# Eight weight sums on VectorE instead of adding DMAs, a PSUM bank for each partial result of a down product, a wider margin in the list scheduler

## The chip, the cores and the metric

One NeuronCore of a Trainium2 chip runs the whole kernel. The metric is the device time of one execution in microseconds. Five engines work side by side, each on its own queue in order: TensorE (PE: matmuls from SBUF into PSUM), VectorE (DVE), ScalarE (ACT), GpSimd (POOL) and SyncE (SP). POOL and SP also issue DMAs: SP the loads and stores, POOL the DMAs that add into SBUF.

## The reference

A gated linear attention over four batches, eight heads, 768 steps and 48 channels, and a bilinear feed-forward layer on its output:

```python
f = 1.0 / (1.0 + np.exp(-f_logit))
for t in range(S):                                  # S = 768
    state = f[:, :, t, :, None] * state + np.einsum('bhd,bhe->bhde', k[:, :, t], v[:, :, t])
    y[:, :, t] = np.einsum('bhd,bhde->bhe', q[:, :, t], state)
x = y.transpose(0, 2, 1, 3).reshape(B * S, H * D)   # 3072 tokens x 384
a = x @ w_a                                         # 384 x 1536
b = x @ w_b
out = (a * b) @ w_out                               # 1536 x 384
```

All matmuls are in fp32. The weights come as doubles and are turned into fp32 on the chip.

## The kernel before

The tokens are cut into eight blocks of 384. A block needs two *units* of attention (four heads each; sixteen units, 0 to 15). Of a unit, DVE makes running products of `f` and scales `q` and `k` (`f_in`, `q_in`, `k_in`; two ACT sigmoids and one POOL step `inv` go ahead of it), PE makes scores (L364), transposes of k (L399), state gains (L423) and the two parts of the output (L466 from the chunk itself, L487 from the states). DVE masks the scores (`at`, L387), ACT copies the transposes (`kT`, L409) and the output (`y`, L512), and SP stores `y` into `xT`, the block's input to the feed-forward layer, and then loads f, k, q and v of the unit three further on.

The feed-forward layer of blocks 0 and 1 is plain: an *up product* (L567) is six matmuls for one of twelve groups of 128 columns, three for b and three for a; ACT copies b, DVE multiplies (L589). For the later blocks the up products are a fast scheme with 15 products for 18 (`up_triples`, L687), and all *down products* (`down`, L780) are one with 7 for 8 in the manner of Strassen and Winograd: two groups of 128 tokens at a time, twelve times in all. Both schemes want sums of weight blocks:

- `combine_w_out`: t1, t2, t4 in the buffer `spare`, and the block b12 of `w_out` changed in place (it is t3);
- `combine_w_ba`: six sums in the buffer `raw` (here called s[0] to s[5]), and after them two blocks of `w_ba`, a31 and a22, changed in place. They may change only when all up products of blocks 0 and 1 are through and when the sums that read them have read them.

These sums are made by ACT, which writes a first term with its sign, and by DMAs of POOL's queue that add one more term each (`add_by_dma`, L599): 20 adding DMAs and 12 ACT copies (L602).

What stands behind what on each engine is decided at build time. `main` holds the feed-forward work in order. Each step has an engine, an assumed duration and, for some, the beat of PE (four matmuls of 164 ns) by which it should be through, its due time. Five lines (`for_out`, `for_x`, `core`, `fore`, `for_ba`) hold the weights' sums on w_out, the sums of x, the units' attention, the work ahead of it, and the weights' sums on w_ba. Before each step of `main`, `fill` puts in what is ready on those lines, unless `delays` finds that a step of `main` on the same engine would come too late for its due time, with `LATENCY` of 200 ns as margin; at marked places a line is emptied up to a point, ready or not.

A down product has four partial results of 192 columns: x0, x1, m0 and m1. PE makes them in the order x0 (3 beats), m1, x0 again (added), x1, m0, x1 anew, m0 again (added). ACT copies x0 to `u` (L797), m1 to `o` (L804) and x0 to `o` (L807); DVE adds the rest. x0 and x1 share one PSUM bank of 512 columns, m0 and m1 another; two down products behind each other take turns with four banks. `up_triples` goes round the same four banks, called v, u, r and t there.

Of the kernel before, what the change touches and what calls it, by code (L numbers as in the profile page):

```python
# [17 lines left out]
ALU = mybir.AluOpType  # L18
# [114 lines left out]
def by_quotients(ctx, tc, q, k, f_logit, v, moe_w_a, moe_w_b, moe_w_out, out, ident, weights, bad):  # L133
    nc = tc.nc
# [26 lines left out]
    for i in range(NSET):  # L161
        t = {n: fixed([128, 2, BLK], f"{n}_in{i}") for n in "qkf"}
# [109 lines left out]
    PE, DVE, ACT, POOL, SP = range(5)  # L272
# [64 lines left out]
    ps_f = [ps_a.tile([128, 512], FP32, tag=f"ps_f{i}", name=f"ps_f{i}") for i in range(4)]  # L337
# [256 lines left out]
    NI, NJ3 = 3, NFT // 3  # L594
    sums_of_w, sums_of_x = {}, {}
    free = list(range(4))
# [4 lines left out]
    def write(to, x, sign):  # L601
        nc.scalar.activation(to, x, AF.Copy, scale=float(sign))  # L602

    def dma_sums(steps, width, issue):


        for to, x, what in steps:
            if what in (1, -1):
                yield ACT, width, 0, write, to, x, what
            else:  # L610
                yield POOL, issue, 3500 if what == "w" else 0, add_by_dma, to, x

    HM = DM // 2
    combos = []
# [5 lines left out]
    def combine_w_out():  # L620

        b11, b12, b21, b22 = (w_out[:, HFT * i:HFT * i + HFT, HM * j:HM * j + HM] for i in range(2) for j in range(2))
        combos.extend(spare.rearrange("p (i n m) -> i p n m", i=3, n=HFT))
        t1, t2, t4 = combos
        combos.insert(2, b12)
        return dma_sums((
            (t1, b11, -1), (t2, b12, -1), (t1, b12, "w"), (b12, b12, -1), (t2, b11, ""), (b12, b22, ""),
            (t2, b22, "w"), (t4, t2, -1), (t4, b21, ""),
        ), 1300, 2500)

    def combine_w_ba():
# [11 lines left out]
        return dma_sums((  # L643
            (s[1], a12, 1), (s[4], a33, -1), (s[5], a11, -1), (s[1], a22, ""), (s[4], a31, ""), (s[5], a31, ""),
            (s[3], a22, 1), (s[2], a12, 1), (s[0], a21, 1), (s[1], a23, ""), (s[4], a21, ""), (s[5], a32, ""),
            (s[3], a23, ""), (s[2], a22, ""), (s[0], a32, ""), (s[3], a32, ""), (s[2], a21, ""),
        ), 1000, 1300), dma_sums((
            (a31, a31, -1), (a31, a11, ""), (a31, a33, "w"), (a22, a31, -1), (a22, s[1], ""), (a22, a13, ""),
        ), 1000, 1300)

    def combine_x(blk):

# [28 lines left out]
    def up_triples(blk):  # L681

        to, tail = products(blk), None
# [25 lines left out]

        for j in range(NJ3):  # L710
            v, u, r, t = (ps_f[i][:, 0:BLK].rearrange("p (g t) -> p g t", g=2) for i in free)
            free[:] = [free[i] for i in (2, 1, 3, 0)]
            c = (sums, last[:, 0:2 * NI * BLK])[j % 2].rearrange("p (g k i t) -> p g k i t", g=2, k=NI, i=2)
            out = {(k, i): c[:, :, k, i] for k in range(NI) for i in range(2)}
            if j % 2:
# [46 lines left out]
    def down(pair):  # L762

        b11, b21, b22 = (w_out[:, HFT * i:HFT * i + HFT, HM * j:HM * j + HM] for i, j in ((0, 0), (1, 0), (1, 1)))
        t1, t2, t3, t4 = combos
# [19 lines left out]
        def times(to, x, w, start=False):  # L785
            for i in range(0, HFT, 2):
                yield on_pe(BEAT, emit, to, x, w, start, i)

        s3 = block()
        yield add(4, s3, a11, a21, ALU.subtract)  # L790
        x, m = (ps_f[i] for i in free[0:2])
        free[:] = free[2:4] + free[1::-1]
        x0, x1, m0, m1 = (t[:, HM * i:HM * i + HM] for t in (x, m) for i in range(2))

        def begin():
            got["u2"] = sb2.tile([128, HM], FP32, tag="u2", name="u2")
# [33 lines left out]
        yield on(ACT, 330, 7, third)  # L830
        s4 = block()
        yield add(10, s4, a12, s2, ALU.subtract)
        yield from times(x1, s2, t2)
        yield on(DVE, 270, 4, sum_u2)
        yield on(DVE, 270, 0, sum_u3)
        yield from times(m0, s1, t1)
        yield on(DVE, 270, 4, last_of, 1, 1, m0)
        yield from times(x1, a22, t4, True)
        yield on(DVE, 270, 8, last_of, 1, 0, x1)
# [54 lines left out]
    with tc.manual_schedule():  # L894
# [200 lines left out]
        def delays(engine, start, load):  # L1095

            with_it, without = start + load, free_at[engine]
            t, beat = now, beats_done
            starts, later = {}, []
            for e, cost, due, *_ in main[done:done + 80]:  # L1100
                if e == PE:
                    beat += 1
                    starts[beat] = t
                    t += cost
                elif e == engine:
                    later.append((t + LATENCY + (0 if due < 1 << 29 or e != DVE else 600), cost, due))
            for ready, cost, due in later:
                if ready >= with_it:
                    return False
                with_it, without = (max(x, ready) + cost for x in (with_it, without))  # L1110
                if with_it + LATENCY > max(starts.get(due, 1 << 30), without + LATENCY):
                    return True
            return False

# [403 lines left out]
```

## Time and profile before

| | us |
|---|---|
| median of 3 runs (lowest, highest) | 648.58 (648.09, 650.92) |
| the profiled execution | 647.26 |
| its span, first to last instruction | 645.1 |
| PE busy, of that span | 579.9 |
| DVE busy | 401.2 |
| ACT busy | 275.9 |
| POOL busy | 87.3 |

PE's mean granted clock was 0.978 of full speed. The profile gives for each instruction its start, its duration, and the idle time of its engine just before it with what ended it. A matmul in fp32 leaves two records, so six matmuls stand as x12. "PEld" are PE's weight loads.

### The profile page before, as it was taken

What the parts mean: (1) busy time and instruction counts of PE and PEld (TensorE: products, weight loads), DVE (VectorE), ACT (ScalarE), POOL (GpSimd) and SP (SyncE); (2) the same over time, 40 slices, a digit from 0 to 9 for tenths busy, and PEclk for the clock granted to TensorE, in tenths of its full rate; (3) what the DMA queues carried; (4) which work ended last, traced back from release to release, by engine and by line L of the source; (5) the groups of instructions that cost most, each with busy time, mean ns of one, the idle gap of its engine ahead of it and who ended that gap; (6) DMA issues with size and microseconds to landing.
All of it is one profiled execution on the core that took longest, in us unless ns stands there. A gap on an engine that the chain in (4) does not pass through costs nothing.

```text
span 645.1 us, 13880 instructions
## 1 busy us (share of the span) xinstructions
PE 579.9 (90%) x5778; PEld 514.2 (80%) x5778; DVE 401.2 (62%) x754; ACT 275.9 (43%) x514; POOL 87.3 (14%) x78
## 2 busy tenths in 40 slices
PE   0859899998727999999999999999999999999995
PEld 0625555556726889989998999989998999999995
DVE  6768445557443959985978676676657246835741
ACT  5577499872203144534543234524441144325300
POOL 5243154455311000000000000000000000000000
PEclk9969999999877999999999999999999999999999
DMA  9886784099995443004300530004000010000000
GB/s 218 230 253 176 179 266 163 2 153 167 181 204 88 117 115 96 3 2 125 86 1 2 134 102 1 1 20 118 1 1 20 32 37 1 1 25 1 2 26 29
DMA packets 38344, 54.47 MB, mean 84 GB/s; under 512 B 4096, under 2 KB 29056, under 8 KB 38272
## 3 DMA queue, kind: packets, MB, share of 16 engines
q1 hardware_dynamic: 29984, 42.38, 24.3%
q0 software_dynamic: 8000, 10.81, 10.8%
q8 instruction: 47, 0.77, 0.5%
q10 hardware_dynamic: 288, 0.30, 0.2%
q14 instruction: 25, 0.20, 0.1%
HBM read 33.23 MB, written 4.72 MB: 59 GB/s over the span
## 4 chain that ended last, share of the span: by engine, by line
PE 72%; DMA 11%; DVE 7%; issue 4%; ACT 3%; SPq 1%; POOL 1%; ACTq 0%; DVEq 0%; POOLq 0%
PE ps_f L687 35%; PE ps_f L780 19%; PE ps_f L567 11%; DMA spare<-w_out 5%; DMA xT<-y 2%; DVE sums L679 2%; DVE groups L679 2%; PE ps_x L423 1%; PE ps_y L466 1%; PE ps_y L487 1%; PE ps_x L364 1%; PE ps_x L399 1%; DMA w_ba<-w_ba 1%; DMA raw<-in_moe_w_a_dram 1%; DVE x_sums L671 1%
## 5 line engine op out<-in xcount | busy, mean ns | idle before, releaser
L567 PE MATMUL ps_f<-xT,w_ba 128*128 128x384 f32 x288 | 99.2, 503 | 7.7 <-DVE w_ba L69 6.0
L567 PEld LDWEIGHTS ps_f<-xT,w_ba 128*128 128x128 f32 x288 | 54.9, 195 | 47.3 <-DVE w_ba L69 7.5
L1166 ACT COPY sums<-ps_f 128x384 f32<-128x384 f32 x120 | 57.5, 479 | 70.5 <-PE ps_f L687 65.7
L1166 ACT COPY groups<-ps_f 128x384 f32<-128x384 f32 x120 | 57.6, 480 | 67.7 <-PE ps_f L687 45.8
L687 PE MATMUL ps_f<-xT,w_ba 128*128 128x192 f32 x384 | 78.4, 327 | 0.0
L780 PE MATMUL ps_f<-w_out,groups 128*128 128x192 f32 x288 | 53.4, 335 | 17.4 <-ACT u L797 17.4
L687 PEld LDWEIGHTS ps_f<-xT,w_ba 128*128 128x128 f32 x384 | 64.9, 190 | 0.2
L780 PEld LDWEIGHTS ps_f<-w_out,groups 128*128 128x128 f32 x288 | 48.5, 195 | 18.8 <-ACT u L797 18.0
L780 PE MATMUL ps_f<-spare,sums 128*128 128x192 f32 x288 | 51.1, 332 | 7.7 <-ACT o L807 7.7
L780 PEld LDWEIGHTS ps_f<-spare,sums 128*128 128x128 f32 x288 | 46.3, 190 | 11.4 <-ACT o L807 11.2
L687 PE MATMUL ps_f<-groups,w_ba 128*128 128x192 f32 x288 | 55.2, 326 | 0.0
L687 PE MATMUL ps_f<-x_sums,raw 128*128 128x192 f32 x288 | 53.8, 331 | 0.8 <-DVE sums L679 0.4
L780 PE MATMUL ps_f<-w_out,sums 128*128 128x192 f32 x288 | 52.6, 329 | 0.0
L687 PEld LDWEIGHTS ps_f<-x_sums,raw 128*128 128x128 f32 x288 | 47.1, 190 | 3.4 <-ACT sums L1166 1.4
L687 PEld LDWEIGHTS ps_f<-groups,w_ba 128*128 128x128 f32 x288 | 48.0, 190 | 0.0
L780 PEld LDWEIGHTS ps_f<-w_out,sums 128*128 128x128 f32 x288 | 47.1, 190 | 0.5
L679 DVE TENSOR_TENSOR sums<-sums,groups 128x768 f32<-128x768 f32 x36 | 34.4, 954 | 21.0 <-ACT groups L1166 20.4
L59 POOL TENSOR_SCALAR sums<-sums 128x768 f32<-128x768 f32 (+1 forms) x20 | 40.1, 2003 | 51.9 <-ACT sums L57 50.2
L297 POOL TENSOR_SCALAR inv<-inv 128x768 f32<-128x768 f32 x14 | 12.8, 913 | 234.9 <-ACT inv L294 234.5
L679 DVE TENSOR_TENSOR sums<-ps_f,sums 128x384 f32<-128x384 f32 x60 | 32.8, 552 | 15.7 <-PE ps_f L687 14.7
L687 PE MATMUL ps_f<-x_sums,w_ba 128*128 128x192 f32 x192 | 40.0, 331 | 1.2 <-ACT groups L1166 1.2
L687 PE MATMUL ps_f<-xT,raw 128*128 128x192 f32 x192 | 39.6, 329 | 0.0
(126 smaller groups left out, 870.8 us busy)
## 6 DMA issues: line engine op xcount, KB each, us to landing
raw<-w_ba POOLq DMA_DIRECT2D x11, 512.0 KB, 10.1
q_in<-in_q_dram SPq DMA_DIRECT2D x32, 144.0 KB, 4.2
k_in<-in_k_dram SPq DMA_DIRECT2D x32, 144.0 KB, 3.7
v_in<-in_v_dram SPq DMA_DIRECT2D x16, 288.0 KB, 4.8
raw<-in_moe_w_out_dram SPq DMA_DIRECT2D x6, 768.0 KB, 4.3
out_dram<-o SPq DMA_DIRECT2D x24, 192.0 KB, 2.3
f_in<-in_f_logit_dram SPq DMA_DIRECT2D x28, 144.0 KB, 3.1
xT<-y SPq DMA_DIRECT2D x46, 72.0 KB, 2.2
```

Of the source, the lines that this page charges most:

```text
L59: nc.gpsimd.tensor_scalar(h, h, HI_MAX, None, ALU.min)
L297: nc.gpsimd.tensor_scalar(inv, inv, EXP_K, 1.0, ALU.mult, ALU.add)
L364: nc.tensor.matmul(ps[h][SUB * p:SUB * p + SUB, o:o + SUB], lhsT=kf[r, tokens(n, c, p)], rhs=qf[r, tokens(n, c, p)], start=True, stop=True,)
L399: nc.tensor.transpose(ps[n][:, c * C:c * C + C], kf[:, o:o + C], ident)
L423: nc.tensor.matmul(ps_x[R * h:R * h + D, p, (n * NC + c) * D:(n * NC + c) * D + D], lhsT=kT[r, n, c, R * h:R * h + D], rhs=t["v"][r, n, c, ...
L466: nc.tensor.matmul(ps[p][e:e + D, o:o + SUB], lhsT=t["v"][r, n, c, h * D:h * D + D], rhs=at[r, h, o:o + SUB], start=o == 0, stop=True, ski ...
L487: nc.tensor.matmul(ps[p][e:e + D, o:o + SUB], lhsT=st[j][r, n], rhs=qf[r, tokens(n, c, p)], start=False, stop=True, skip_group_check=True,)
L567: nc.tensor.matmul(ps[nm][:, 0:BLK], lhsT=w[:, kt, ft * 128:ft * 128 + 128], rhs=xT[blk][:, kt], start=kt == 0, stop=kt == NKT - 1,)
L679: nc.vector.tensor_tensor(to, x, y, op)
L687: nc.tensor.matmul(ps[:, g], lhsT=sums_of_w[name][:, g, 128 * j:128 * j + 128], rhs=sums_of_x[blk][name], start=start and g == 0, stop=Tru ...
L780: nc.tensor.matmul(to, lhsT=x[:, i // 2, i % 2], rhs=w[:, NI * (i % 2) + i // 2], start=start and i == 0, stop=i == HFT - 1, skip_group_ch ...
L1166: do(*args)
```

## The change

Eight sums are now single tensor-tensor instructions of DVE, each with two inputs: four on w_out (with other signs and in another order, so that each is one addition or subtraction) and four on a31 and a22. Nine adding DMAs and six ACT copies that made them are no longer there. The 6 copies and 11 adding DMAs for s[0] to s[5] stay. The scheduler's assumed duration of a new sum is 1270 and 1150 ns, and an adding DMA no longer counts for 3500 ns behind its issue. In `down` each of x0, m1, x1, m0 is the first 192 columns of a bank of its own, the same four banks for each down product; two matmul groups that wrote into a half that was already marked as started now start their own bank. The last turn of `up_triples` leaves the banks in another order. In `delays` the margin is twice `LATENCY`.

```diff
-    def dma_sums(steps, width, issue):
+    def w_sums(steps, width):
         for to, x, what in steps:
             if what in (1, -1):
                 yield ACT, width, 0, write, to, x, what
+            elif what == "+":
+                yield POOL, 1300, 0, add_by_dma, to, x
             else:
-                yield POOL, issue, 3500 if what == "w" else 0, add_by_dma, to, x
+                yield DVE, width + 200, 0, nc.vector.tensor_tensor, to, x, *what
...
-        return dma_sums((
-            (t1, b11, -1), (t2, b12, -1), (t1, b12, "w"), (b12, b12, -1), (t2, b11, ""), (b12, b22, ""),
-            (t2, b22, "w"), (t4, t2, -1), (t4, b21, ""),
-        ), 1300, 2500)
+        return w_sums((
+            (t1, b12, (b11, ALU.subtract)), (t2, b22, (t1, ALU.subtract)),
+            (t4, b21, (t2, ALU.subtract)), (b12, b22, (b12, ALU.subtract)),
+        ), 1070)
...
-            (a31, a31, -1), (a31, a11, ""), (a31, a33, "w"), (a22, a31, -1), (a22, s[1], ""), (a22, a13, ""),
-        ), 1000, 1300)
+            (a31, a11, (a31, ALU.subtract)), (a31, a31, (a33, ALU.add)),
+            (a22, s[1], (a31, ALU.subtract)), (a22, a22, (a13, ALU.add)),
+        ), 950)
...
-            free[:] = [free[i] for i in (2, 1, 3, 0)]
+            free[:] = [free[i] for i in ((2, 1, 3, 0) if j < NJ3 - 1 else (2, 3, 1, 0))]
...
-        x, m = (ps_f[i] for i in free[0:2])
-        free[:] = free[2:4] + free[1::-1]
-        x0, x1, m0, m1 = (t[:, HM * i:HM * i + HM] for t in (x, m) for i in range(2))
+        x0, m1, x1, m0 = (ps_f[i][:, 0:HM] for i in free)
...
-        yield from times(x1, s2, t2)
+        yield from times(x1, s2, t2, True)
...
-        yield from times(m0, s1, t1)
+        yield from times(m0, s1, t1, True)
...
-                if with_it + LATENCY > max(starts.get(due, 1 << 30), without + LATENCY):
+                if with_it + 2 * LATENCY > max(starts.get(due, 1 << 30), without + 2 * LATENCY):
```

Two lines are gone in `down` and two more stand above, so L687 and L780 are L689 and L782 in the new kernel, L671 and L679 are L673 and L681, and the lines from L797 on keep their numbers. The new sums are recorded at L1125, where the scheduler emits a line's step.

On POOL, from the first adding DMA on. A name is what an instruction writes, then what it reads; `inv` is the step ahead of a unit's scans; a wait names the engine or the DMA lane (DMASW are the adding DMAs'). Before:

```order
L599 DMA spare<-w_out 128x6x192 [waits Activation_49]
L297 TENSOR_SCALAR inv<-inv 128x768 [waits Activation_49]
L599 DMA raw<-w_ba 128x2x512 [waits DMAHW5_49,DMAHW7_49,DMAHW0_49,Activation_49]
L599 DMA raw<-w_ba 128x2x512 [waits DMAHW5_49,DMAHW4_49,DMAHW6_49,DMAHW2_49,Activation_49]
L599 DMA raw<-w_ba 128x2x512 [waits Activation_49]
L599 DMA spare<-w_out 128x6x192
L599 DMA w_out<-w_out 128x6x192 [waits Activation_49]
L599 DMA spare<-w_out 128x6x192 [waits DMASW4_49]
L297 TENSOR_SCALAR inv<-inv 128x768 [waits Activation_49]
L599 DMA raw<-w_ba 128x2x512 [waits DMASW1_49]
L599 DMA raw<-w_ba 128x2x512 [waits DMASW2_49,DMASW0_49]
L599 DMA raw<-w_ba 128x2x512 [waits DMASW3_49]
```

and now:

```order
L297 TENSOR_SCALAR inv<-inv 128x768 [waits Activation_49]
L599 DMA raw<-w_ba 128x2x512 [waits DMAHW5_49,DMAHW7_49,DMAHW0_49,Activation_49]
L599 DMA raw<-w_ba 128x2x512 [waits DMAHW5_49,DMAHW4_49,DMAHW6_49,DMAHW2_49,Activation_49]
L599 DMA raw<-w_ba 128x2x512 [waits Activation_49]
L599 DMA raw<-w_ba 128x2x512 [waits DMASW0_49]
L599 DMA raw<-w_ba 128x2x512 [waits DMASW1_49]
L297 TENSOR_SCALAR inv<-inv 128x768 [waits Activation_49]
L599 DMA raw<-w_ba 128x2x512 [waits DMASW2_49]
L599 DMA raw<-w_ba 128x2x512 [waits DMAHW1_49]
L599 DMA raw<-w_ba 128x2x512 x2
L599 DMA raw<-w_ba 128x2x512 [waits DMASW6_49]
L599 DMA raw<-w_ba 128x2x512 [waits DMASW7_49]
```

The DMAs on `spare`, `w_out` and (further down) `w_ba` are gone; unit 5's `inv` now stands behind five adding DMAs, where it stood behind seven, and the next unit's behind all eleven.

On ACT, from the end of the first down product to the third. `L602` are the weights' copies, `u` and `o` the down product's, L294 and L291 a unit's sigmoids. Before:

```order
L807 COPY o<-ps_f_105 128x192
L294 ACTIVATE inv,tails<-f_in_79,less 128x768
L291 ACTIVATE f_in_79<-f_in_79 128x768
L602 ACTIVATE w_ba<-w_ba 128x2x512
L409 COPY kT<-ps_x 128x768
L512 COPY y<-ps_y 128x6x64
L512 COPY y<-ps_y 48x6x64 x2
L602 ACTIVATE w_ba<-w_ba 128x2x512
L797 COPY u_1419<-ps_f_107 128x192
L804 COPY o<-ps_f_108 128x192
L807 COPY o<-ps_f_107 128x192
L294 ACTIVATE inv,tails<-f_in_83,less 128x768
```

and now:

```order
L294 ACTIVATE inv,tails<-f_in_79,less 128x768
L291 ACTIVATE f_in_79<-f_in_79 128x768
L807 COPY o<-ps_f_105 128x192
L409 COPY kT<-ps_x 128x768
L512 COPY y<-ps_y 128x6x64
L512 COPY y<-ps_y 48x6x64 x2
L797 COPY u_1439<-ps_f_105 128x192
L294 ACTIVATE inv,tails<-f_in_83,less 128x768
L291 ACTIVATE f_in_83<-f_in_83 128x768
L804 COPY o<-ps_f_106 128x192
L409 COPY kT<-ps_x 128x768
L807 COPY o<-ps_f_105 128x192
```

The copies of `w_ba` no longer stand ahead of `u`; the sigmoids of f_in_83 moved from behind the second down product's copies to between its `u` and `o`.

On DVE, around the last up products of blocks 0 and 1 (L589 are their products, f_in_83 and start belong to unit 4's scans). Before:

```order
L589 TENSOR_TENSOR groups<-ps_f_108,x_sums 128x3x128
L589 TENSOR_TENSOR groups<-ps_f_106,x_sums 128x3x128
L301 SCALAR_TENSOR_TENSOR f_in_83<-f_in_83,zero 128x384 x2
L304 TENSOR_TENSOR held<-f_in_83,least 128x2
L589 TENSOR_TENSOR groups<-ps_f_108,x_sums 128x3x128
L309 RECIPROCAL start<-f_in_83 128x4
```

and now:

```order
L589 TENSOR_TENSOR groups<-ps_f_108,x_sums 128x3x128
L1125 TENSOR_TENSOR spare<-w_out 128x1152
L1125 TENSOR_TENSOR spare<-w_out,spare 128x1152 x2
L1125 TENSOR_TENSOR w_out<-w_out 128x6x192
L589 TENSOR_TENSOR groups<-ps_f_106,x_sums 128x3x128
L301 SCALAR_TENSOR_TENSOR f_in_83<-f_in_83,zero 128x384 x2
L304 TENSOR_TENSOR held<-f_in_83,least 128x2
L309 RECIPROCAL start<-f_in_83 128x4
```

The four sums on w_out stand in one row between two products and ahead of unit 4's scans. The four on w_ba come later: the first between unit 5's `k_in` and its mask, the second behind unit 6's `k_in`, the third behind unit 6's mask, the fourth behind unit 7's `k_in`. The third reads s[1] from `raw` and waits for adding DMAs. On PE the scores of unit 4 stand two matmuls of up products (four of 192 columns) earlier than before, those of unit 5 ten down matmuls earlier; from the first down product of the third block on, PE's row is the same as before but for bank numbers.

More of the change, by code (lines that the diff above doesn't have):

```diff
@@ L642, in combine_w_ba @@
         )
[L643 to L647, printed above, removed]
-            (a31, a31, -1), (a31, a11, ""), (a31, a33, "w"), (a22, a31, -1), (a22, s[1], ""), (a22, a13, ""),
-        ), 1000, 1300)
+        return w_sums((
+            (s[1], a12, 1), (s[4], a33, -1), (s[5], a11, -1), (s[1], a22, "+"), (s[4], a31, "+"), (s[5], a31, "+"),
+            (s[3], a22, 1), (s[2], a12, 1), (s[0], a21, 1), (s[1], a23, "+"), (s[4], a21, "+"), (s[5], a32, "+"),
+            (s[3], a23, "+"), (s[2], a22, "+"), (s[0], a32, "+"), (s[3], a32, "+"), (s[2], a21, "+"),
+        ), 1000), w_sums((
+            (a31, a11, (a31, ALU.subtract)), (a31, a31, (a33, ALU.add)),
+            (a22, s[1], (a31, ALU.subtract)), (a22, a22, (a13, ALU.add)),
+        ), 950)
     def combine_x(blk):
```

## The prediction

> **What bounds the kernel now.** I read the page's first two parts, then the work of two stages, then who TensorE (PE) waited for, then the timeline around the longest waits.
>
> ```profile
> span 645.1 us, 13880 instructions
> PE 579.9 (90%) x5778; PEld 514.2 (80%) x5778; DVE 401.2 (62%) x754; ACT 275.9 (43%) x514; POOL 87.3 (14%) x78
> ...
> 129.10:231.90 102.80, 79.61 (x976) 66.63 (x975) 59.64 (x130) 31.60 (x54) 29.07 (x25) 0.92 0.83 143
> 231.90:645.10 413.20, 399.06 (x3815) 384.53 (x3813) 264.92 (x482) 151.88 (x328) 6.29 (x7) 1.00 0.15 38
> ```
>
> The stage rows give start and end, length, then busy time (instructions) of PE, weight loads, DVE, ACT, POOL, then granted clock, DMA share and GB/s. PE is the busiest engine, idle for 65.2 us of the span. The first 129.1 us hold code that the change does not touch. In the second stage (129.1 to 231.9: the weights' sums, the first three down products) PE is idle for 102.8 - 79.6 = 23.2 us, and nobody else is busy for more than 59.6. In the third it is idle for 14.1 us, some 6 of them the tail after the last matmul. Who it waited for, in the whole span and after 205 us:
>
> ```profile
> PE ps_f L780 <- ACT u L797: 17.4, 2, 15.3
> ...
> PE ps_f L780 <- ACT o L807: 7.7, 12, 1.1
> ...
> PE ps_f L780 <- DMA spare<-w_out: 3.9, 1, 3.9
> ```
> ```profile
> PE ps_f L780 <- ACT o L807: 6.9, 10, 1.1
> PE ps_f L687 <- ACT groups L1166: 1.2, 1, 1.2
> PE ps_f L687 <- DVE sums L679: 0.4, 1, 0.4
> PE ps_f L687 <- DVE groups L679: 0.4, 1, 0.4
> ```
>
> 17.4 + 3.9 + 0.8 + 1.1 (two and one of the twelve L807 waits) make the 23.2 us of the second stage. The timeline shows where they come from:
>
> ```profile
> 156.00 1.16 ACT L602 ACTIVATE spare<-spare 128x1152 f32<-128x1152 f32 x1 [7.01 <-DMA spare<-w_out]
> 157.43 2.22 PE L780 MATMUL ps_f<-w_out,groups 128*128 128x192 f32 x12 [2.10 <-ACT u L797]
> 169.13 1.24 PE L780 MATMUL ps_f<-spare,groups 128*128 128x192 f32 x4 [3.86 <-DMA spare<-w_out]
> 176.91 1.21 POOL L599 DMA_DIRECT2D w_ba<-w_ba  x1
> 188.89 1.19 POOL L599 DMA_DIRECT2D w_ba<-w_ba  x1 [10.77 <-DMA w_ba<-w_ba]
> 196.05 1.06 ACT L602 ACTIVATE w_ba<-w_ba 128x1024 f32<-128x1024 f32 x1 [19.51 <-DMA w_ba<-w_ba]
> 197.36 3.62 PE L780 MATMUL ps_f<-w_out,groups 128*128 128x192 f32 x12 [15.30 <-ACT u L797]
> ```
>
> One mechanism three times: an adding DMA of the weights is late. At 157 and 197 us an ACT copy of the same chain waits for it, and the copy `u` of the second down product, which has nothing to do with the weights' sums, stands behind it in ACT's queue; PE waits for `u`. At 169 PE itself waits for a sum. The adding DMAs are late since they queue behind each other:
>
> ```profile
> q0 software_dynamic: 7783, 10.40, 79.0%
> ...
> raw<-w_ba POOLq DMA_DIRECT2D x11, 512.0 KB, 10.1
> spare<-w_out POOLq DMA_DIRECT2D x4, 576.0 KB, 9.4
> ```
>
> Between 120 and 205 us POOL's queue alone took 79% of the 16 DMA engines (67 us of them, some 3.4 us for each of the 20 adding DMAs), and one landed 9 to 10 us after its issue. After the two long gaps PE also runs at half clock:
>
> ```profile
> 199.00:200.00 1.00, 1.00 (x5) 1.00 (x4) 0.00 (x0) 0.00 (x0) 0.00 (x0) 0.50 0.93 162
> 201.00:202.00 1.00, 0.61 (x4) 0.61 (x4) 0.00 (x0) 0.98 (x2) 0.00 (x0) 1.00 1.00 170
> 213.56 2.11 PE L780 MATMUL ps_f<-w_out,groups 128*128 128x192 f32 x12
> ```
>
> The twelve matmuls at 197.36 took 3.62 us, where twelve of the same kind take 2.11: 1.5 us lost. The clock was 0.50 at 170 us too, after the gap of 3.86, so I put the two gaps at 2 x 1.5 = 3.0 us. (The gap of 2.10 us left the clock alone: its twelve took 2.22.)
>
> **The change, part by part.**
>
> *Nine adding DMAs and six ACT copies go.* All five on w_out and all four on the first weights' own blocks leave POOL's queue, and with them every DMA that ACT or PE waited for in the rows above. Gain: 17.4 + 3.9 us of waits and 3.0 of slow clock. ACT loses four copies of 1152 columns (1.16 us in the row at 156.00) and two of 1024 (1.06): 6.8 us, off the path. The eleven adds of `raw` stay. The first was issued at 132.6 us behind copies that now stand a little earlier, at an estimated 131; with 3.4 to 4.0 us each the eighth lands at 158 to 163 us.
>
> *Eight sums come onto DVE.* Prices from the groups:
>
> ```profile
> L679 DVE TENSOR_TENSOR sums<-sums,groups 128x768 f32<-128x768 f32 x36 | 34.4, 954 | 21.0 <-ACT groups L1166 20.4
> L679 DVE TENSOR_TENSOR groups<-sums 128x1152 f32<-128x1152 f32 x12 | 16.3, 1357 | 10.0 <-ACT sums L1166 10.0
> ```
>
> 1152 columns: 1.357 us; 1024, two thirds of the way from 768: 954 + 0.67 x 403 = 1.22. Sum 4 x 1.357 + 4 x 1.22 = 10.3 us. Four of them, on w_out, now come between two up products:
>
> ```profile
> 117.66 25.00 PE L567 MATMUL ps_f<-xT,w_ba 128*128 128x384 f32 x77
> 128.57 0.56 DVE L589 TENSOR_TENSOR groups<-ps_f,x_sums 128x384 f32<-128x384 f32 x1 [1.86 <-PE ps_f L567]
> 132.44 0.56 DVE L589 TENSOR_TENSOR groups<-ps_f,x_sums 128x384 f32<-128x384 f32 x1 [3.31 <-PE ps_f L567]
> 140.66 0.95 DVE L318 TENSOR_TENSOR k_in<-k_in,inv 128x768 f32<-128x768 f32 x1
> ```
>  An up product is twelve of PE's records, 25.00 x 12 / 77 = 3.9 us. DVE's work in the stage becomes 59.6 + 10.3 = 69.9 us. PE's own need is 79.6 - 3.0 = 76.6, so PE stays the longer one, but DVE is then over 85% full and its order matters. Following the new order with these durations: the four w_out sums start behind the product of 128.57 us and end near 134.5; the product of 132.44 is then some 2 us late, less than the 3.9 us of the up product that runs before its bank is wanted again. Unit 4's scans follow, and its `k_in` is ready near 141.5, as before (141.6), while its scores now stand two matmuls (1.3 us) earlier on PE: about 1 us of new wait. Three of the sums on w_ba stand just behind a unit's `k_in`, the first ahead of its mask too: 1.22 + 0.95 us on DVE, where PE has the scores and four matmuls to do, some 2.2 us: covered, with a tenth to spare. They wait for adding DMAs 2 and 3 (landing near 143, reached near 157) and 8 (158 to 163, reached near 175): covered.
>
> *Moved steps.* ACT now has the next unit's two sigmoids ahead of copy `o` in the second down product and ahead of `u` in the third, and the first sigmoid waits for that unit's f load, which SP issues behind five stores to xT; the second output store of the first down product now stands behind that unit's loads, and the next copy into `o` (one buffer) waits for it.
>
> ```profile
> 178.07 7.33 SPq L531 DMA_DIRECT2D xT<-y  x5
> 209.04 3.06 SPq L531 DMA_DIRECT2D xT<-y  x5
> 239.04 0.93 ACT L294 ACTIVATE inv<-f_in,less 128x768 f32<-128x768 f32 x1 [2.88 <-DMA f_in<-in_f_logit_dram]
> 240.48 0.92 PE L687 MATMUL ps_f<-x_sums,w_ba 128*128 128x192 f32 x4 [1.18 <-ACT groups L1166]
> ```
>
> The last two rows show this very wait costing PE 1.18 us. I take 1 us here; the ends are 0 and 4.3 us a place (five issues in 7.33 instead of 3.06). With the 1 us of unit 4: 2.0 us of new waits in the stage.
>
> [...]
>
> ```profile
> 204.11 1.48 DVE L301 TENSOR_TENSOR_SCAN f_in<-f_in,zero 128x384 f32<-128x384 f32 x1
> 203.96 0.82 POOL L297 TENSOR_SCALAR inv<-inv 128x768 f32<-128x768 f32 x1
> 246.96 0.94 DVE L301 TENSOR_TENSOR_SCAN f_in<-f_in,zero 128x384 f32<-128x384 f32 x1
> ```
>
> The scan took 1.48 us instead of 0.94 while POOL worked. [...]
>
> *Banks.* Each down product runs x0, m1, x0 and then x1; x1 shared x0's bank and so waited for the copy of x0:
>
> ```profile
> 615.60 0.32 ACT L807 COPY o<-ps_f 128x192 f32<-128x192 f32 x1 [1.63 <-PE ps_f L780]
> 615.97 4.17 PE L780 MATMUL ps_f<-spare,sums 128*128 128x192 f32 x24 [0.41 <-ACT o L807]
> 613.28 0.96 DVE L679 TENSOR_TENSOR sums<-sums,groups 128x768 f32<-128x768 f32 x1
> ```
>
> With a bank of its own it needs only its operand, which DVE ended at 614.24, 1.3 us before PE was let through to it. All 7.7 us should go; 1.9 are in the stage's 23.2, so 5.8 more. What is late next: the next down product reuses the four banks at once, but in the same order, so each has a whole product (some 14 us) to be read.
>
> *Wider margin.* It can take the other 2.0 us of waits after 205 us, or put side work off until it is forced; beyond the first downs of the third stage PE's row of work is the same as before. I take 0.5 us (ends: +2.0 and -1.2, the longest wait of this kind).
>
> **Sum.** 23.2 + 3.0 - 2.0 + 5.8 + 0.5 = 30.5 us. The profiled execution took 647.26 us (2.2 around its span of 645.1): 616.8. The median of the runs, 648.58, would give 618.1. I say 617.
>
> **Rivals.**
> - *DVE becomes the bound.* For: 69.9 of some 78 us, and scores, masks and scans of four units pass through it in order. Against: its pieces are covered by matmuls at each place I followed. If all 10.3 us land on the path: 617 + 8 to 10 = 625 to 627.
> - *ACT held by a load.* Five slow issues on SP (7.33 us) push the f load past the point where PE wants `kT` or `u`, at one place or two: 621 to 626. Against: they were slow while adding DMAs filled the DMA engines, which now ends near 175 us.
> - *The banks give nothing*, since x1 then waits for its operand or m0 for a read: 5.8 + 1.1 back, 624. Against: the row of 613.28.
> - *The stall only changes engine*: DVE, not ACT, stands before a late adding DMA. 15.3 + 1.5 back: 634. Against: 12 us between landing and use.
> - *Slower*: the same wait, at the sum that reads `raw` and waits for the eighth adding DMA, with masks and `u` sums behind it. It decides once that DMA lands 34 us after DVE gets there, after 209 us (the gain of 31 and the 3.2 us named below), or 9.8 us for each of the eight one behind the other. The median of 10.1 us from issue to landing speaks for it, but that was with several in flight.
>
> **How the numbers follow.** Likeliest 0.63 (own range 611 to 622); DVE bound 0.13; ACT held 0.12; no bank gain 0.04; stall on another engine 0.04; slower 0.04, a quarter of it within 0.5%. The floor, with no new wait and 2.0 from the margin, is 30.5 + 3.5 = 34.0 off 647.3 or 648.6: 613 to 615; I go to 611 for what slow clock and queues may hold beyond it. The top, 630, takes in both DVE and ACT rivals nearly together. 0.5% is 3.2 us, about what a measurement of this kernel can tell from no change.
>
> **What would show it.** Right: between 129 and 232 us no wait of PE over 3 us, none of ACT for an adding DMA, granted clock 1.00 throughout; the first L689 matmul (the up products) near 207 us instead of 231.9; no PE wait for the `o` copy of L807 in any of twelve down products; eight DVE instructions at L1125 of 1.2 to 1.4 us. Wrong: a PE wait for `kT`, `u` or a scores operand of over 4 us, which would lower the clock again, or DVE idle before L1125 on a DMA.

## The result: 609.35 us, below the predicted range

| | before | after |
|---|---|---|
| median, us (lowest, highest; 4 runs each) | 648.35 (648.09, 650.92) | 609.35 (608.74, 610.66) |
| ratio, 95% interval | | 0.9393 (0.9363 to 0.9422) |
| the profiled execution | 647.26 | 608.74 |
| its span | 645.1 | 606.9 |

The prediction was 617, with a range of 611 to 630: the direction and the mechanism held, and the gain, 39.0 us by the medians, was sized too small at 30.5. Two later sets of five runs gave medians of 610.32 (built with the old margin, which leaves the order of instructions as it is) and 609.74, below the range too.

First the page of the new kernel, then its two stages by the view of stretches (columns as in the prediction), cut at its own first L689 matmul (the up products, L687 before):

```profile
span 606.9 us, 13866 instructions
PE 571.9 (94%) x5778; PEld 511.7 (84%) x5778; DVE 408.3 (67%) x762; ACT 269.8 (44%) x508; POOL 75.0 (12%) x69
...
129.10:204.72 75.62, 74.09 (x1017) 63.27 (x1016) 68.10 (x139) 23.48 (x44) 15.95 (x15) 1.00 0.67 134
204.72:606.90 402.18, 395.19 (x3768) 384.31 (x3766) 262.42 (x478) 152.00 (x328) 5.83 (x7) 1.00 0.15 38
```

The stage of the weights' sums took 75.6 us where it took 102.8, PE idled in it for 1.5 us where it had idled for 23.2, and the clock was 1.00 throughout. The third stage is shorter too, by 11 us. All that PE waited for behind 129 us (total, times, longest, in us):

```profile
PE ps_x L423 <- ACT kT L409: 1.5, 1, 1.5
PE ps_f L689 <- DVE groups L681: 0.4, 1, 0.4
PE ps_f L689 <- ACT sums L1166: 0.3, 1, 0.3
```

No wait for `u`, for a DMA into `spare`, or for the `o` copy of L807 is left. The new sums, in the view of their line:

```profile
L1125 DVE TENSOR_TENSOR w_ba<-w_ba x3: 1218/1219/1221, 154.2 to 186.3; 128x1024 f32<-128x1024 f32 x3
L1125 DVE TENSOR_TENSOR spare<-w_out,spare x2: 1357/1358/1358, 128.5 to 129.9; 128x1152 f32<-128x1152 f32 x2
```

Durations are min/median/max in ns: 1.36 and 1.22 us, as the prediction took from the groups of other additions.

**Where the 38.2 us of span come from.** I compared the two traces at the same point of PE's work. At the first down product:

```profile
150.25 0.81 PE L780 MATMUL ps_f<-w_out,groups 128*128 128x192 f32 x4
149.36 2.11 PE L782 MATMUL ps_f<-w_out,groups 128*128 128x192 f32 x12
```

The first row is before, the second after. The new kernel has done unit 4's L466 step (0.82 us from its start to the next) by then, the old one has not: 0.89 + 0.82 = 1.7 us gained. At the first up product of the scheme:

```profile
231.86 0.81 PE L687 MATMUL ps_f<-x_sums,raw 128*128 128x192 f32 x4
204.72 0.81 PE L689 MATMUL ps_f<-x_sums,raw 128*128 128x192 f32 x4
```

27.14, and 0.82 for the next unit's L466, which again only the new kernel has done: 28.0 us. So 1.7 us came before any changed matmul, 26.3 between the two points (the prediction's sum for them was 23.2 + 3.0 - 2.0 = 24.2), and 38.2 - 28.0 = 10.2 behind them (6.3).

What the prediction missed is seen at one bank wait, in the last down product. Before, then after:

```profile
628.09 2.11 PE L780 MATMUL ps_f<-w_out,groups 128*128 128x192 f32 x12
...
630.61 4.17 PE L780 MATMUL ps_f<-spare,sums 128*128 128x192 f32 x24 [0.41 <-ACT o L807]
...
634.62 2.11 PE L780 MATMUL ps_f<-spare,groups 128*128 128x192 f32 x12
```
```profile
590.63 2.11 PE L782 MATMUL ps_f<-w_out,groups 128*128 128x192 f32 x12
592.58 4.06 PE L782 MATMUL ps_f<-spare,sums 128*128 128x192 f32 x24
596.48 2.11 PE L782 MATMUL ps_f<-spare,groups 128*128 128x192 f32 x12
```

The same 36 records (two to a matmul, so a beat is four of them) take 634.62 - 628.09 = 6.53 us and 596.48 - 590.63 = 5.85. The wait shows 0.41 us of idle time and cost 0.68. The other 0.27: a group of matmuls that follows without a wait starts 0.16 us before the modelled end of the one ahead (592.58 against 590.63 + 2.11), and behind a wait the first group is 0.11 longer (4.17 against 4.06). The idle time shown is so a lower bound of what this wait cost.

| us | predicted | measured |
|---|---|---|
| PE's waits of the stage | 23.2 | 23.2 |
| slow clock | 3.0 | 3.3 (what is left of the stage's 26.3; 3.2 by the rows of the clock below) |
| new waits | -2.0 | -1.8 (1.53 + 0.27) |
| the other nine bank waits, idle time | 5.8 | 5.8 |
| restart behind the 15 waits, 15 x 0.27 | none | 4.0 (1.6 in the stage, 2.4 behind it) |
| margin; measured: the small waits at L687, 2.0 - 0.7 of idle time and one restart | 0.5 | 1.6 |
| before the first down product | none | 1.7 |
| not assigned | | 0.4 |
| sum | 30.5 | 38.2 |

The 0.27 was measured at one bank wait; that it holds for the other waits is tested in experiments 2 and 3 for the bank waits, and assumed for the three others. The slow clock can be read on its own, from the old trace's rows (the clock stands ahead of the DMA share):

```profile
169.00:170.00 1.00, 0.87 (x4) 0.90 (x5) 0.00 (x0) 0.00 (x0) 0.00 (x0) 0.76 1.14 197
170.00:172.00 2.00, 2.00 (x10) 1.91 (x9) 0.00 (x0) 0.31 (x1) 0.00 (x0) 0.50 1.11 193
172.00:173.00 1.00, 1.00 (x5) 1.00 (x4) 0.00 (x0) 0.49 (x1) 0.97 (x1) 0.53 1.09 188
...
200.00:201.00 1.00, 0.98 (x5) 0.69 (x4) 0.00 (x0) 0.00 (x0) 0.00 (x0) 0.88 1.12 193
```

A mean of 0.76 is half clock for 0.48 of that microsecond, and so on: it was half from 169.52 to 172.94 us, all of it with PE at work, and behind the long gap PE worked at half clock from 197.36 to 200.24. Half of 3.42 and of 2.88 is 3.2 us.

### The profile page after: what moved, and what is told of

Its sections match the earlier page's. It is cut to its first block, busy times and chain, and to the rows that moved or that the text cites. A ratio compares the mean times of both kernels' runs of the same rounds, so it can differ in the third digit from the quotient of the medians.

```text
span 606.9 us, 13866 instructions
## 1 busy us (share of the span) xinstructions
PE 571.9 (94%) x5778; PEld 511.7 (84%) x5778; DVE 408.3 (67%) x762; ACT 269.8 (44%) x508; POOL 75.0 (12%) x69
## 3 DMA queue, kind: packets, MB, share of 16 engines
q0 software_dynamic: 2992, 5.77, 5.6%
## 4 chain that ended last, share of the span: by engine, by line
PE 91%; DMA 4%; SPq 1%; ACT 1%; DVE 1%; issue 1%; ACTq 0%
PE ps_f L689 39%; PE ps_f L782 27%; PE ps_f L567 15%; PE ps_y L466 2%; PE ps_y L487 2%; PE ps_x L364 2%; PE ps_x L423 2%; DMA f_in<-in_f_logit_dram 1%; PE ps_x L399 1%; DMA xT<-y 1%; DMA k_in<-in_k_dram 1%; DMA out_dram<-o 1%; SPq L215 1%; SPq L211 0%; PE ps_f L487 0%
## 5 line engine op out<-in xcount | busy, mean ns | idle before, releaser
L689 PE MATMUL ps_f<-xT,w_ba 128*128 128x192 f32 x384 | 78.4, 327 | 0.0
L689 PEld LDWEIGHTS ps_f<-xT,w_ba 128*128 128x128 f32 x384 | 64.9, 190 | 0.2
L689 PE MATMUL ps_f<-groups,w_ba 128*128 128x192 f32 x288 | 55.2, 326 | 0.0
L689 PE MATMUL ps_f<-x_sums,raw 128*128 128x192 f32 x288 | 53.7, 330 | 0.6 <-DVE groups L681 0.4
L782 PE MATMUL ps_f<-w_out,sums 128*128 128x192 f32 x288 | 52.5, 328 | 0.0
L782 PE MATMUL ps_f<-w_out,groups 128*128 128x192 f32 x288 | 51.8, 329 | 0.0
L782 PE MATMUL ps_f<-spare,sums 128*128 128x192 f32 x288 | 50.0, 327 | 0.0
L689 PEld LDWEIGHTS ps_f<-x_sums,raw 128*128 128x128 f32 x288 | 47.1, 190 | 2.8 <-ACT sums L1166 1.7
L689 PEld LDWEIGHTS ps_f<-groups,w_ba 128*128 128x128 f32 x288 | 48.0, 190 | 0.0
L782 PEld LDWEIGHTS ps_f<-w_out,groups 128*128 128x128 f32 x288 | 47.2, 190 | 0.8
L782 PEld LDWEIGHTS ps_f<-w_out,sums 128*128 128x128 f32 x288 | 47.1, 190 | 0.4
L782 PEld LDWEIGHTS ps_f<-spare,sums 128*128 128x128 f32 x288 | 46.9, 190 | 0.3
L681 DVE TENSOR_TENSOR sums<-sums,groups 128x768 f32<-128x768 f32 x36 | 34.4, 955 | 17.4 <-ACT groups L1166 16.9
L681 DVE TENSOR_TENSOR sums<-ps_f,sums 128x384 f32<-128x384 f32 x60 | 32.9, 553 | 15.7 <-PE ps_f L689 14.7
L689 PE MATMUL ps_f<-x_sums,w_ba 128*128 128x192 f32 x192 | 39.9, 330 | 0.0
L689 PE MATMUL ps_f<-xT,raw 128*128 128x192 f32 x192 | 39.5, 328 | 0.0
```

What stands on the lines that cost most here:

```text
L681: nc.vector.tensor_tensor(to, x, y, op)
L689: nc.tensor.matmul(ps[:, g], lhsT=sums_of_w[name][:, g, 128 * j:128 * j + 128], rhs=sums_of_x[blk][name], start=start and g == 0, stop=Tru ...
L782: nc.tensor.matmul(to, lhsT=x[:, i // 2, i % 2], rhs=w[:, NI * (i % 2) + i // 2], start=start and i == 0, stop=i == HFT - 1, skip_group_ch ...
```

## Experiments

Each was timed beside runs of the kernel before; times are medians, intervals 95%.

**1. The margin alone, on either kernel.** Two runs of one idea: take the margin out of the new kernel, put it into the old one.

```diff
-                if with_it + 2 * LATENCY > max(starts.get(due, 1 << 30), without + 2 * LATENCY):
+                if with_it + LATENCY > max(starts.get(due, 1 << 30), without + LATENCY):
```

> The new kernel with the old margin in the list scheduler. Its instructions stand in the same order on all five engines, with the same waits, as in the new kernel, so theory A says that this is a second run of one program: 609.4, within 0.3%, and the wait of 1.2 us at L687 that went was not taken by the margin. The rival, the term of +0.5 us on record with its ends of -1.2 and +2.0, would have 607.4 to 610.6 here and no way to do it. What the run is for besides: how far the untouched first 129 us and the few small waits behind 205 us differ between two runs of one program.

> The kernel before with the wider margin alone. The order of the instructions and their waits are the same as before, so theory A says 648.4, and that its trace is a second one of the program before: the first down product would then be reached within some 2 us of 150.25 us, and if it lies 1.5 to 2 us earlier, as in the trace after, those 1.9 us of the gain are chance between runs and not the change. Rival: 646.5, if the margin worked.

Measured: 610.32 us for the new kernel with the old margin (0.9412, 0.9395 to 0.9428), 648.26 for the old one with the new (1.0005, 0.9993 to 1.0018). The order of instructions is the same with either margin on all five engines, so the two runs show how far two executions of one program differ. The first down product was reached at 151.68 us here, at 149.36 in the trace after and at 150.25 in that of after_again (experiment 7); in the old program at 149.21 and 150.25, or 150.0 and 151.1 with the L466 step added. The 1.7 us of the table lie within that scatter, so the change cannot be credited with them. The waits at L687 stayed gone without the margin (0.25 and 0.38 us are left) and stayed put with it (1.59, 0.43 and 0.38 us).

**2. The banks alone, on the kernel before** (b_banks).

```diff
...
-        x, m = (ps_f[i] for i in free[0:2])
-        free[:] = free[2:4] + free[1::-1]
-        x0, x1, m0, m1 = (t[:, HM * i:HM * i + HM] for t in (x, m) for i in range(2))
+        x0, m1, x1, m0 = (ps_f[i][:, 0:HM] for i in free)
...
```

> The kernel before with the four PSUM banks of the new kernel alone; the weight sums stay with the adding DMAs. Theory A (from the trace after): a wait of PE costs the idle time that the profile shows for it and 0.27 us more (0.16 of overlap with the matmul ahead that is lost, 0.11 of a longer first matmul). Twelve waits of 7.7 us together are then worth 7.7 + 12 x 0.27 = 10.9 us; one of 0.41 + 0.27 stands ahead of a wait for a DMA that lands when it lands, so about 10.2 us off: 638.2. Rival B (the prediction's way of counting): 7.7 - 0.4 = 7.3 us off, 641.1. Rival C: the banks give nothing without the sums, 648.4. In the trace: no PE wait for the copy o of L807 by A and B.

Measured: 637.50 us (0.9837, 0.9818 to 0.9857), 11.0 off (9.3 to 11.8 by the interval; 9.8 between the two traces). Theory A's 638.2 is inside the interval, B's 641.1 (0.9886) is not. The stretch behind the first up product:

```profile
229.90:635.30 405.40, 396.76 (x3816) 384.87 (x3814) 264.64 (x482) 152.09 (x328) 6.31 (x7) 1.00 0.15 39
```

It took 645.10 - 231.86 = 413.24 us before. 7.84 us went, although the small waits at L687 grew by 0.3: 8.14 us for nine waits with 5.77 us of shown idle time, so 0.26 us above it for each.

**3. One of the two shared banks brought back into the new kernel.** First x1 in x0's bank (a_x1_shared), then m0 in m1's (a_m0_shared).

```diff
-        x0, m1, x1, m0 = (ps_f[i][:, 0:HM] for i in free)
+        x0, m1, m0 = (ps_f[i][:, 0:HM] for i in (free[0], free[1], free[3]))
+        x1 = ps_f[free[0]][:, HM:2 * HM]
...
```
```diff
+        x0, m1, x1 = (ps_f[i][:, 0:HM] for i in free[0:3])
+        m0 = ps_f[free[1]][:, HM:2 * HM]
...
```

> The new kernel, but x1 is the second half of x0's bank, as before; m0 keeps its own. Theory A (idle shown and 0.27 us for each restart): at least 12 x 0.68 = 8.2 us back, and up to 10.9 where ACT is late with the copy: 617.5 to 620.3. Rival B (only the idle shown): 12 x 0.41 to 7.7, so 614.3 to 617.1.

> The new kernel, but m0 is the second half of m1's bank, as before; x0 and x1 keep banks of their own (three banks in use). Theory A: only x1 waited, because its first matmul comes right behind the second part of x0, whose copy has not been made; m0 comes 24 matmuls (3.9 us) behind the next product and m1 has long been read: 609.4. Rival B: any two partial results in one bank cost a wait of 0.68 us each, 12 x 0.68 = 8.2: 617.5.

Measured: 622.36 us with x1 in x0's bank (0.9605, 0.9578 to 0.9632) and 610.09 with m0 in m1's (0.9408, 0.9383 to 0.9434). The whole effect of the banks is x1's; m0's own bank is worth nothing that can be measured. B is refuted, and A fell short by 2 us. Behind the first up product A holds: 409.84 us against 402.18 of the new kernel, 7.66 for nine waits of 5.79, one small wait less. The rest was in the stage, at 178 us, in this execution (624.29 us, above the median; the lowest of the six runs took 621.02):

```profile
178.63 2.93 PE L782 MATMUL ps_f<-spare,sums 128*128 128x192 f32 x8 [3.10 <-ACT o L808]
...
178.00:186.00 8.00, 7.37 (x95) 6.79 (x96) 2.12 (x7) 2.01 (x5) 0.00 (x0) 0.50 0.01 2
186.00:188.00 2.00, 2.00 (x8) 2.00 (x7) 1.59 (x7) 0.00 (x0) 0.00 (x0) 0.53 0.28 74
```

L808 is the third copy there (L807). It stands behind kT and a copy `o` on ACT, both late, so the bank wait became 3.10 us long, and the clock fell to half for ten microseconds (eight records took 2.93 us, against 1.47 to 1.57 at full clock).

**4. The eight sums alone**, with the old banks and margin (b_dve).

```diff
...
-                yield POOL, issue, 3500 if what == "w" else 0, add_by_dma, to, x
+                yield DVE, width + 200, 0, nc.vector.tensor_tensor, to, x, *what
...
```

> The kernel before with the eight sums on VectorE alone; the old banks, the old margin. Theory A: the waits for u and for the DMA into spare go (17.4 + 3.9 us, three restarts of 0.27, slow clock of 3.3), and one wait of 1.8 for kT comes: 23.6 off, 624.8; the banks' waits stay at twelve. Rival B (the sum on record): 21.3 + 3.0 - 2.0 = 22.3 off, 626.1. Rival D: the whole kernel's gain of 39 came from the sums, 609 to 612. Rival E: the two parts need each other (the bank waits push other steps), under 20 off, over 628.

Measured: 622.88 us (0.9620, 0.9601 to 0.9639), 25.6 off; its runs spread from 619.64 to 625.08. Theory A's 624.8 is 0.9635, inside the interval, and B's 626.1 (0.9655) just outside it. A's wait for `kT` did not come: with the old banks PE waited there for the copy `o` (below). D and E are refuted: sums and banks are nearly separate gains, 25.6 + 11.0 = 36.6 of the 38 to 39. The part that needs both is the place of experiment 3:

```profile
178.41 1.57 PE L782 MATMUL ps_f<-spare,sums 128*128 128x192 f32 x8 [2.90 <-ACT o L809]
```

With the old banks PE stands there for 2.90 us, with the new ones 1.53 for kT.

**5. Half of the sums back to adding DMAs**, in the new kernel: those on `w_ba`, then those on `w_out`.

```diff
...
-            (a31, a11, (a31, ALU.subtract)), (a31, a31, (a33, ALU.add)),
-            (a22, s[1], (a31, ALU.subtract)), (a22, a22, (a13, ALU.add)),
+            (a31, a31, -1), (a31, a11, "+"), (a31, a33, "w"), (a22, a31, -1), (a22, s[1], "+"), (a22, a13, "+"),
```
```diff
...
-            (t1, b12, (b11, ALU.subtract)), (t2, b22, (t1, ALU.subtract)),
-            (t4, b21, (t2, ALU.subtract)), (b12, b22, (b12, ALU.subtract)),
+            (t1, b11, -1), (t2, b12, -1), (t1, b12, "w"), (b12, b12, -1), (t2, b11, "+"), (b12, b22, "+"),
+            (t2, b22, "w"), (t4, t2, -1), (t4, b21, "+"),
```

> The new kernel, but the two changed blocks of w_ba are made as before, by two ACT copies and four adding DMAs; the sums on w_out stay on VectorE. Theory A (the queue): the adds were late because 20 of them queued behind each other; with 15 left each lands some 5 us after its issue, ACT waits for 3 to 8 us, PE less, since its next copy u is not wanted at once: 611 to 617. Rival B (the chain): a link of an ACT copy and two adds takes 20 us whatever else is in the queue, so that the wait of 15.3 us and 1.5 of slow clock come back: 625 to 627.

> The new kernel, but the sums on w_out are made as before, by four ACT copies and five adding DMAs; those on w_ba stay on VectorE. Theory A: the waits of 2.10 and 3.86 us, two restarts and 1.8 of slow clock come back, 8.3 us: 617.7. Rival B: VectorE now stands before the eighth adding DMA, which lands five DMAs (17 us) later than in the new kernel, with masks and sums behind it: 622 to 632, and a wait of VectorE for raw in the trace.

Measured: 626.12 us (0.9659, 0.9634 to 0.9684) and 622.54 (0.9618, 0.9592 to 0.9644). In the first, ACT's and PE's timelines:

```profile
172.38 1.06 ACT L602 ACTIVATE w_ba<-w_ba 128x1024 f32<-128x1024 f32 x1 [11.39 <-DMA w_ba<-w_ba]
...
174.84 1.53 PE L466 MATMUL ps_y<-at,v_in 64*48 64x64 f32 x48 [7.29 <-ACT y L512]
...
191.27 1.12 PE L423 MATMUL ps_x<-v_in,kT 64*48 64x48 f32 x38 [4.54 <-ACT kT L409]
```

ACT waited 11.4 us for the chain where it had waited 19.5 before. The two adds behind each other took 10.4 and 5.0 us from issue to landing, where they had taken 11.7 and 7.1: with five DMAs fewer in the queue the chain is only 3.4 us shorter, and the rest of the difference is that ACT came to its wait later in the chain. So A is refuted. The time is B's, its account is not: PE no longer waited for `u` but for `y` and `kT`, 11.8 us in all, and the clock was at half behind both (0.50 from 172 to 180 us, a mean of 0.55 from 190 to 195). The second kernel's waits, behind 129 us:

```profile
PE ps_f L782 <- DMA spare<-w_out: 2.9, 1, 2.9
PE ps_f L782 <- ACT u L797: 2.1, 1, 2.1
PE ps_f L782 <- DVE o L816: 1.2, 1, 1.2
PE ps_f L689 <- DVE sums L681: 1.0, 2, 0.6
PE ps_f L689 <- DVE groups L681: 0.9, 1, 0.9
PE ps_f L689 <- ACT sums L1166: 0.7, 1, 0.7
PE ps_f L689 <- ACT groups L1166: 0.7, 1, 0.7
```

The waits of 2.13 us for `u` and 2.86 for `spare` are back, as A said, and VectorE did not wait for `raw` (B refuted, though the time lies in its range). It was still 5 us over A's 617.7. The trace (an execution of 621.06) shows why: behind 200 us, where the sums on `w_ba` now ran up to 212 us, PE had five small waits of 0.56 to 1.19 us for VectorE and ACT, 4.06 us together and 1.35 for restarts. Added up against the new kernel's trace: 2.13 + 2.86 + 0.54 for the two waits and their restarts, 3.4 for two stretches of half clock (157.07 to 160.48 and 167.31 to 170.72 us), 5.4 for the small waits, less 0.5 and 1.8 for the waits of 0.25 and 1.53 us that it no longer has, make 12.0 us; the spans differ by 619.0 - 606.9 = 12.1. That the late sums on `w_ba` cause the small waits was not tested apart.

**6. VectorE's share doubled**: behind each sum one more instruction of its size.

```diff
                 yield DVE, width + 200, 0, nc.vector.tensor_tensor, to, x, *what
+                yield DVE, width + 200, 0, nc.vector.tensor_tensor, to, to, to, ALU.max
```

> The new kernel with each of the eight sums followed by one more VectorE instruction of the same size that leaves the values as they are (the maximum of the sum with itself): 10.3 us more of VectorE in the stage, 78.4 us of work in a stage that took 75.6. Theory A (VectorE has some 7 us to spare there): VectorE becomes the bound by 3 to 5 us, 612 to 615. Rival B (the sums hide nowhere, each microsecond lands on the path): 619.7. Rival C (VectorE is far from bounding): 609.4 to 610.5.

Measured: 611.50 us (0.9439, 0.9419 to 0.9460), 1.2 to 2.2 above the three medians of the new kernel, between A and C. B is refuted. A's reason fell too:

```profile
129.10:205.70 76.60, 75.50 (x945) 64.40 (x947) 69.78 (x131) 23.81 (x44) 17.83 (x15) 1.00 0.65 131
```

VectorE was busy for 69.8 us of this stretch and not for 78.4: the planner knew the costs and put work off. The sums on `w_ba` and their doubles themselves ran from 164.6 to 207.7 us, where the new kernel's four had run from 154.2 to 187.5, and behind the first L690 matmul, at 202.31 us, VectorE was busy for 273.6 of 406.8 us, where it had been for 262.4 of 402.2. So the run shows that this scheduler finds room for twice the load, not that VectorE could take it in the old places. That VectorE bounds nothing in the new kernel itself is seen in the waits of its trace: 0.4 us of PE's is for VectorE.

**7. The one wait that is left.** In the new kernel ACT's timeline ahead of the wait of 1.53 us:

```profile
173.27 0.94 ACT L294 ACTIVATE inv<-f_in,less 128x768 f32<-128x768 f32 x1 [3.52 <-DMA f_in<-in_f_logit_dram]
...
176.77 0.32 ACT L804 COPY o<-ps_f 128x192 f32<-128x192 f32 x1 [1.59 <-DMA out_dram<-o]
176.98 0.81 ACT L409 COPY kT<-ps_x 128x768 f32<-128x768 f32 x1
```

Two things hold `kT`: the load of f and the output store, both late on SP. I moved the second output store of the first down product to POOL's queue, and in a second kernel also the load of f ahead of the stores into xT; the new kernel ran once more beside that one.

```diff
...
+        if u >= NQ:
+            load_unit(u + NSET, "f")
...
-            load_unit(u + NSET)
+            load_unit(u + NSET, "kqv")
...
+            queue = nc.gpsimd if pair[0] == (0, 1) and i == 0 else nc.sync
...
```

> The new kernel, with the second output store of the first down product issued by POOL and not by SP, where it stands behind the loads of a unit. Theory A: the only long wait of PE left behind 129 us (1.53 us for kT at 177.84, and 0.27 of restart) comes from the copy o on ACT, which waits for this store to have read its one buffer; it goes, 1.8 us off: 607.6. Rival B: ACT is held by the load of f all the same (its sigmoid ran at 173.27 behind an idle time of 3.5 us), and kT is still late: 609.4. Rival C: POOL's store is slower to land than SP's and holds o for longer: over 611.

> The new kernel with the second output store of the first down product on POOL's queue, and with a unit's load of f issued ahead of the five stores into xT instead of behind them. Theory A: of the wait for kT, 0.75 us was left with the store on POOL, since the sigmoid of f waited for its load, issued at 169.58 behind 3.05 us of stores; it goes: 1.8 us under the new kernel, 607.6 to 608.5, and no PE wait over 0.5 us behind 129 us. Rival B: the stores into xT, now 1.1 us later, hold the sums of x on VectorE and PE waits there: 609.4 or more. Rival C: below what a run tells from the new kernel, though the trace shows the wait gone.

> The new kernel once more, as the yardstick of the run beside it and for the spread between runs of one program: 609.4 to 610.3, with the first down product reached between 149.3 and 151.7 us, the range of the seven traces so far that stand on the new sums.

Measured: 608.88 us with the store moved (0.9392, 0.9368 to 0.9416), its wait for kT down to 0.75; with both, 608.36 (0.9395, 0.9380 to 0.9410), and 609.74 for the new kernel in the same job (0.9425, 0.9409 to 0.9441). With both, this is all PE waited for behind 129 us:

```profile
PE ps_f L691 <- DVE groups L683: 0.4, 1, 0.4
```

The mechanism is shown. The time, 1.4 us below the new kernel's on the same chip, has an interval that touches the other's (0.941), so that it is likely but not certain to be faster than the new kernel; from the one with the store alone it cannot be told apart.

## Why the prediction was right in kind and too small in size

- *The stall at the adding DMAs*: right. 17.4 + 3.9 us of waits went with the sums, no copy of ACT waits for an adding DMA, and experiment 5 brings waits back with either half. Its size was right but for the restarts. The reason given, that the adds queue behind each other, is the smaller part for the sums on `w_ba`: with five fewer in the queue the two adds ahead of ACT's copy still took 15.4 us of 18.8. Each waits for the one ahead to land (in the kernel before, POOL stood for 10.77 us ahead of the second); why such an add takes 5 us or more stays open.
- *Slow clock, 3.0*: right; 3.3 remained for it, and 3.2 is read from the clock itself.
- *VectorE, 10.3 us on eight instructions*: right to 0.01 us each, and covered. The rival of 0.13 did not come: 0.4 us of PE's waits is for VectorE. Unit 4's scores, for which I had put 1 us, did not wait. The sums do not wait for an adding DMA either (the rivals of a stall on another engine and of a slower kernel).
- *ACT held by a load*: right in place; its 1 us was 1.53 + 0.27 at `kT`, behind f's load and the store for `o`, the two things of SP's queue that the prediction named. That the 2.0 us for all new waits came out at 1.8 is luck: one half of it was nothing, the other nearly twice its size.
- *Banks, "All 7.7 us should go"*: the waits did go, but the term was mis-sized. It took the idle time shown as the price; nine of them cost 8.1 us with 5.8 shown (b_banks), and by 0.27 each the twelve of 7.7 come to 10.9. (b_banks gained 11.0 by the medians and 9.8 by the traces, with a wait for `spare` that grew by 0.7; 10.2 was expected.) This, with the restart of the three other waits, is the step that failed: 4.0 of the missing 7.7 us. With it the forecast would have been 613, 4 us above the measured. Of the other 3.7, 1.7 is scatter ahead of the first down product, 1.1 the small waits at L687, and 0.9 the rest of the table. That only x1's bank counts (experiment 3) agrees with the prediction, which named x1 alone.
- *Margin, +0.5*: no such effect exists. The edit moves no instruction, as the two orders of instructions would have told before. The small waits at L687 did shrink (1.6 us), and the sums did it: they shrank in b_dve (to 0.6 us) and stayed in b_banks (2.3). By which steps was not followed; side work that the sums displaced is likely.
- *The range's lower end*: 611 was the sum with no new wait and a little more. It had no room for what two executions of one program differ by before 150 us (2.3 us between the two traces of the new kernel), nor for a price that is above the idle time.
- *The scan of 1.48 us beside POOL's step*, where another took 0.94: it was no term of the sum, and whether a weights' sum beside such a step takes longer too was not tested, since none of POOL's `inv` steps (126.15, 140.55, 155.48, 174.38 and 188.21 us) ran beside one. The issue of three adding DMAs on POOL, 128.21 to 132.07, did lie beside the four on `w_out`, and these took 1.35 to 1.36 us each, no more than the row they were priced from.

## What to carry to other kernels

A copy on ACT that waited for a DMA held up what stood behind it: before, its wait of 19.5 us kept `u` back, and PE stood for 15.3. So a sum on an engine with room can be worth several times its own cost: here 10 us of VectorE for 25 us of the whole. Price a wait of PE above the idle time that the profile shows (here 0.68 us for 0.41), by comparing the start-to-start time of the same matmuls with and without the wait, and multiply by how often it recurs. Look at which of two partial results in one PSUM bank is written right behind the other's last matmul; here only that one was worth a bank of its own (622.36 us with x1's shared, 610.09 with m0's).

## What the hardware showed that I had not expected

The granted clock fell to half for some 3.41 us or for a whole multiple of it. In the old kernel with the new margin, behind a wait of 2.14 us that ended at 156.43:

```profile
156.43 3.23 PE L780 MATMUL ps_f<-w_out,groups 128*128 128x192 f32 x12 [2.14 <-ACT u L797]
...
157.00:158.00 1.00, 1.00 (x7) 1.00 (x6) 1.00 (x2) 0.00 (x0) 1.00 (x2) 0.73 1.11 190
...
160.00:161.00 1.00, 0.93 (x3) 0.93 (x4) 0.00 (x0) 0.97 (x4) 1.00 (x2) 0.56 1.10 158
161.00:162.00 1.00, 1.00 (x8) 1.00 (x7) 0.00 (x0) 1.00 (x2) 0.81 (x1) 1.00 1.04 170
```

Between them it was 0.50. A mean of 0.73 is half clock for 0.54 of that microsecond and 0.56 for 0.88 of it: 0.54 + 2 + 0.88 = 3.42 us. By the same sum it was 3.42 us in the old kernel behind its wait of 3.86, and in x1's kernel (3.10) 10.24, three times 3.41. The length of the gap alone does not tell: behind 2.14 us it fell here, and behind 2.10 it did not in another execution of the same program; behind 3.10 it fell in a_x1_shared, and behind 2.90 at the same place it did not in b_dve. Where the gap lies fits better. The changes of clock in this trace, read in this way (157.46, 160.87, 167.70, 171.11, 184.77 and 201.83 us), lie whole multiples of 3.413 us apart (44.37 us from the first to the last, thirteen times that), to 0.02 us, and so do the four that the old kernel's trace has between 129 and 640 us (169.52, 172.94, 186.60 and 200.24). Marked off in steps of that length from these points, the old kernel's trace has, from 100 us to the last matmul, two steps at full clock with more than 1.55 us of PE's idle time in all: one with 3.02 and one with 3.41. Half clock followed these two and none of the others. It followed steps with 2.14, 2.03 and 3.41 us of idle time in the old kernel with the new margin, with 2.0 and 2.8 in a_wout_dma, and with 2.11 of the gap of 3.10 in a_x1_shared. The gap of 2.10 lay across an edge, with 1.55 us in one step. The 2.90 of b_dve cannot be placed so: its clock was 1.00 throughout from 150 to 205 us. How long the clock then stays at half (one step, three behind the 3.10, four and five behind the gaps of 15.3) was not settled.

At half clock eight records took 2.93 us, against 1.47 to 1.57 at full clock. Estimated from these rows, the stretches of 3.42 and 10.24 us cost 1.7 and up to 5.1 us on top of their waits, half of each; the gaps of 2.10 and 2.90 us cost nothing of the kind. That may be why b_dve's runs spread over 5.4 us and the new kernel's over 1.9. The mean clock on record fits in part (0.975 in the slowest of b_dve's runs, 0.986 in the fastest, but 0.985 in one 3 us slower than that); it was not tested.
